# VectorE's order inside a visit: both masked copies, then the two steps of the turn back, then both row maxima

## The chip, the cores and the metric

The kernel runs on one core of one Trainium2 chip. The metric is the device time of one execution in microseconds. TensorE (PE in the profile) multiplies matrices, VectorE (DVE), ScalarE (ACT) and GpSimd (POOL) work on tiles element by element, and SyncE (SP) issues the transfers. Each engine takes its own instructions in order; across engines an instruction waits for a semaphore that another one raises.

## The reference

Four layers follow each other: a Fourier mixing layer, an attention layer, and the same two again. The change lies in the attention layer, `_B_ref`: 2048 rows of 640 numbers, 32 heads of 20, and each query sees itself and the 255 keys ahead of it.

```python
scores = jnp.einsum("bhqd,bhkd->bhqk", q, k) * (Dh ** -0.5)
mask = (idx[:, None] - idx[None, :] >= 0) & (idx[:, None] - idx[None, :] < W)   # W = 256
scores = jnp.where(mask[None, None], scores, -1e9)
p = _softmax(scores, axis=-1)
o = jnp.einsum("bhqk,bhkd->bhqd", p, v)
return (lambda x, *d: x.transpose(*d))(o, 0, 2, 1, 3).reshape(B, S, D) @ wo
```

## The kernel before

The queries are cut into 16 tiles of 128 rows. A query tile meets three key tiles: its own (near), the one ahead of it (near), and the one two ahead (far), of which only the part inside the window counts. Attention runs in *visits*, numbered G. A visit takes one query tile and four heads, in two halves `pi` of two heads each, and it works on several stages of different visits at once:

- `scores(G, ...)` on TensorE: the scores by query of this visit. The near ones go into the tiles sq (one for each half; `near` in the code), the far ones into the first quarter of the tiles sk (`farq`).
- `by_key(G - 8)` on TensorE: the scores of an earlier visit once more, by key, into the other three quarters of sk (`tps`).
- `largest(G, pi)` on VectorE: a masked copy (`copy_predicated`, line 1155) puts the far scores where the own tile's scores are masked; a row maximum (`tensor_reduce`, line 1157) over sq gives m.
- `probabilities(G - 8, pi)` on ScalarE: an activation of sk gives ptq (line 1210), first the half 1, then the half 0; GpSimd then masks it (lines 1214 and 1216).
- `part_tops` on GpSimd, at odd G: splits m into tops. `hand_on`, at odd G: TensorE turns the tops, ScalarE copies them out as ht (line 1175).
- `values`, at odd G: TensorE multiplies ptq with v; ScalarE copies the sums out as pvs (line 1242).
- `back(n)`, at even G from 12 on: the turn back. TensorE transposes pvs, VectorE takes a reciprocal r (line 1258) and a product o (line 1259), GpSimd splits o into two halves os (lines 1261 and 1262).
- a *fill unit* on TensorE at the end of most visits: 15 matmuls of a projection, of the output product or of the next layer. Their sums share two buffers, pf, with the turns and the values, and other engines evict them (the output product's by VectorE, line 935).
- single steps of layer norms on VectorE, let in by `slow_step` behind the last row maximum (`topped`).

So an even visit holds the turn back, and an odd visit the tops and the values. TensorE's order is the order of the code: each of its instructions is issued behind the one before. On VectorE, `in_line("dve")` issues an instruction behind the one noted last in `marks["dve"]`. What is not tied so (norm steps, evictions) is placed between by a scheduler when the program is built.

Of the kernel before, what the change touches and what calls it, by code (L numbers as in the profile page):

```python
# [72 lines left out]
def body(ctx: ExitStack, tc: tile.TileContext, x_in, cmat, whid, wqkv, wo, out):  # L73
# [750 lines left out]
    def attention(layer, proj, dst, final):  # L824
        with ExitStack() as st:
# [295 lines left out]
            @contextmanager  # L1121
            def in_line(name):
                with ExitStack() as order:
                    if name in marks:
                        order.enter_context(tc.issue_after(marks[name]))
                    yield
# [6 lines left out]
            def scores(G, which):  # L1133
# [3 lines left out]
                for a in which:  # L1137
# [4 lines left out]
                    for e in range(2):  # L1142
                        for pi in range(2):
                            r = slice(64 * pi, 64 * pi + 3 * DH + 2)
                            o = farq[pi][:, e] if a == 0 else near[pi][:, e, a % 2]
                            matmul(o, qs[r, p0 + e, t0:t0 + P], KS[kt // 2][r, p0 + e, k0:k0 + P], start=True, stop=True)

            def largest(G, pi):
                i, p0 = place(2 * G)
                n, k = divmod(G, 2)  # L1150
                if k == 0 and pi == 0:
                    TOP[n] = sb.tile([P, 2, 2, 2], F32, tag="m", name="m", bufs=3)
                far = farq[pi] if i >= 2 else neg[:, None, :].to_broadcast([P, 2, P])
                with in_line("dve"):
                    marks["dve"] = nc.vector.copy_predicated(near[pi][:, :, 0], mask[:, None, :].to_broadcast([P, 2, P]), far).ins  # L1155
                with in_line("dve"):
                    marks["dve"] = nc.vector.tensor_reduce(TOP[n][:, pi, :, k], near[pi][:, :, :1 + (i >= 1)], axis=AX.XY, op=OP.max).ins  # L1157
                topped[0] = marks["dve"]

            def part_tops(n):  # L1160

                m = TOP.pop(n).rearrange("p l e k -> p l (e k)")
                f = sb.tile([P, 2, 4], F32, tag="mf", name="mf", bufs=2)
                hl = tops[n % 2].rearrange("p (l h c) -> p l h c", l=2, h=2)
                nc.gpsimd.tensor_scalar(f, m, -1.0 / M_UP, None, op0=OP.mult)
                nc.gpsimd.tensor_copy(hl[:, :, 0], f)
                nc.gpsimd.tensor_tensor(hl[:, :, 1], f, hl[:, :, 0], op=OP.subtract)
# [76 lines left out]
            def back(n):  # L1244
                b, k = divmod(n, NP // 2)
                t = PVS.pop(n)
                pv = new_f().rearrange("p (a b) -> p a b", a=4)
                for m in range(2):
                    transpose(pv[:, 2 + m], t[:, m], idf)
                pbv = pv[:, 2:].rearrange("p m (h e) -> p (m h) e", e=32)  # L1250
                if k == 0:
                    flush(("out", b - 3))
                    OS[b] = sb.tile([P, 2, 2, D], F16, tag="os", name="os", bufs=3)
                r = sb.tile([P, 8], F32, tag="r", name="r", bufs=2)
                cs = slice(4 * k * DH, 4 * (k + 1) * DH)
                o = sb.tile([P, 2, 4 * DH], F32, tag="o", name="o", bufs=2)
                hi, lo = (OS[b][:, :, m, cs] for m in range(2))
                nc.vector.reciprocal(r, pbv[:, :, DH])
                nc.vector.tensor_tensor(o.rearrange("p m (h e) -> p (m h) e", e=DH), pbv[:, :, :DH],  # L1259
                                        r.unsqueeze(2).to_broadcast([P, 8, DH]), op=OP.mult)  # L1260
                nc.gpsimd.tensor_copy(hi, o)
                nc.gpsimd.tensor_tensor(lo, o, hi, op=OP.subtract)
                last = b == NBQ - 1
                d1 = (k + 1) * 4 * DH // P
                if last and d1 > k * 4 * DH // P and (d1 > 2 or k > LAST_FROM):
                    for m in range(2):
                        step0 = max(now[0] + LAST_STEPS[0], NG + 2 * KEY_LAG if m else LAST_STEPS[1] if d1 < ND else 0)
                        fill.append(Unit(step0, last_out(2 * b + m, lastd[0], d1), "last", NS + 2 * d1 + m, [(2 * b + m - 2, 2)]))
                    lastd[0] = d1
                elif k == NP // 2 - 1 and not last:  # L1270
                    for m in range(2):
                        i = 2 * b + m
                        at, due, kind = now[0] + OUT_STEPS[0] + OUT_STEPS[2] * m, 2 * NP * (b + 2) + OUT_STEPS[1], ("out", b)
                        need = [(i - 2, 2)] if i > 1 else []
                        outs.append((at, need, partial(out_turn, i)))
                        fill.append(Unit(at, out_tile(i), kind, due + 3 * m + 2, [(i, 1)] + ["wo"] * (layer == 0)))
# [38 lines left out]
            for G in range(NS // 2 + 1):  # L1315
                now[0] = g = 2 * G
                b, r = divmod(g, 2 * NP)
                if g == NG:
                    floor.append(loads[-1])
                if g < NG:  # L1320
                    if r == 0:
                        flush(("qk", b))
                        if b == 0:
                            queue_qk(1)
                            queue_v(1)
                keyed = 0 <= G - KEY_LAG < NG // 2
                if g < NG:
                    scores(G, (0,))
                if keyed:
                    by_key(G - KEY_LAG)  # L1330
                if g < NG:
                    scores(G, (2, 1))
                if g < NG:
                    largest(G, 0)
                if keyed:
                    probabilities(G - KEY_LAG, 1)
                if g < NG:
                    largest(G, 1)
                    if G % 2:
                        part_tops(G // 2)  # L1340
                if keyed:
                    probabilities(G - KEY_LAG, 0)
                n = due(G, HAND_LAG)
                if n is not None:
                    hand_on(n)
                n = due(G, BACK_LAG)
                if n is not None:
                    with in_line("dve"):
                        back(n)
                c = 2 if g == 0 else b + 3  # L1350
                if g < NG and c < NBQ and (g == 0 or r == X2_STEP):
                    wanted.append(c)
                if wanted and x2s and g >= x2s[0] + 4 * (g > 0):
                    slow.append(rows_norm(wanted.pop(0), x2s.pop()))
                    x2s.clear()
                if slow:
                    normed_at[0] = g
                if wanted and not slow and not x2s and g >= normed_at[0] + FREE_STEPS:
                    x2s += [g, [keep.tile([P, D], F32, tag="res0", name="x2", bufs=2) for t in range(2)]]
                    for t in range(2):  # L1360
                        load(x2s[1][t], x2_d[2 * wanted[0] + t])
                if g < NG and r == ROWS_STEP:
                    flush(("v", b))
                    if b < NBQ - 2:
                        proj.new_rows(b + 2)
                        queue_qk(b + 2)
                        queue_v(b + 2)
                if g < NG and r == HIDDEN_STEP:
                    if b == NBQ - 1 and not final:
                        flush(("v", b))  # L1370
                        hidden = Hidden(xu_d)
                        pieces = hidden.pieces()
                        for k in range(2):
                            fill.append(Unit(g + NEXT_STEPS[k], hidden.stage(k, None), "next", NG + k))
                for _ in range(STEPS[layer][G % 2]):
                    slow_step()
                run_later()
                for _ in range(PIECES):
                    next(pieces, None)
                while handed and handed[0][0] <= now[0]:  # L1380
                    handed.popleft()[1]()
                run_held(1 << 20)
                if outs and outs[0][0] <= g and all(done.get(k, 1 << 20) + FREE_STEPS <= g for k in outs[0][1]):
                    outs.pop(0)[2]()
                n = due(G, VALUE_LAG)
                if n is not None:
                    for part in range(2):
                        values(n, part)
                if not (G % 2 and NG - 2 * NP <= g < THIN_TO[layer]):
                    run_unit(G % 2 == 0)  # L1390
                if G % 2 and g < NG and left() and 2 * left() > must_to() - r:
                    run_unit()
# [40 lines left out]
```

## Time and profile before

| | us |
|---|---|
| median of three runs | 2076.37 (2076.05 to 2076.40) |
| the profiled execution's own time | 2078.21 |
| its span, first to last instruction | 2076.4 |
| TensorE busy | 1996.0 |
| VectorE busy | 1552.9 |
| masked copies, line 1155, 448 + 64 | 189.7 + 33.5 |
| row maxima, line 1157, 512 | 345.4 |
| reciprocals, line 1258, 128 | 25.3 |
| products o, line 1259, 128 | 40.8 |

A row of the timeline reads: start, duration, engine, line, operation, output <- input with shapes, count; in brackets the idle time of the engine ahead of it and what ended it. A row of the waits reads: who waited <- for whom: us in total, times, longest. A row of the stretches reads: from and to, length, and the busy time of TensorE, its weight loads, VectorE, ScalarE and GpSimd with their instruction counts, then granted clock, share of the DMA engines, and GB/s. The ends of matmuls are modelled in the trace.

### The profile page before, as it was taken

What the parts mean: (1) busy time and instruction counts of PE and PEld (TensorE: products, weight loads), DVE (VectorE), ACT (ScalarE), POOL (GpSimd) and SP (SyncE); (2) the same over time, 40 slices, a digit from 0 to 9 for tenths busy, and PEclk for the clock granted to TensorE, in tenths of its full rate; (3) what the DMA queues carried; (4) which work ended last, traced back from release to release, by engine and by line L of the source; (5) the groups of instructions that cost most, each with busy time, mean ns of one, the idle gap of its engine ahead of it and who ended that gap; (6) DMA issues with size and microseconds to landing.
All of it is one profiled execution on the core that took longest, in us unless ns stands there. A gap on an engine that the chain in (4) does not pass through costs nothing.

```text
span 2076.4 us, 55961 instructions
## 1 busy us (share of the span) xinstructions
PE 1996.0 (96%) x21881; PEld 1452.4 (70%) x21881; DVE 1552.9 (75%) x3261; ACT 1114.1 (54%) x1971; POOL 1471.0 (71%) x2162
## 2 busy tenths in 40 slices
PE   7999999999999999999999999999999999999998
PEld 4777777776767776777667777777677677777765
DVE  8888778767688788766638779787777877776673
ACT  5444555534256666666654444444342666666664
POOL 5777788868458778765557778777783677776654
PEclk9999999999999999999999999999999999999999
DMA  7556467565554444443635455454845454543322
GB/s 271 182 200 207 159 216 237 169 254 193 141 107 118 109 109 117 98 102 91 175 131 175 159 174 183 149 171 144 298 146 131 92 124 106 128 110 88 85 74 71
DMA packets 280509, 311.11 MB, mean 150 GB/s; under 512 B 107572, under 2 KB 214836, under 8 KB 271156
## 3 DMA queue, kind: packets, MB, share of 16 engines
q1 hardware_dynamic: 279668, 306.88, 49.9%
q8 instruction: 171, 2.80, 0.6%
q14 instruction: 94, 0.77, 0.1%
q10 hardware_dynamic: 576, 0.66, 0.1%
HBM read 201.72 MB, written 83.46 MB: 137 GB/s over the span
## 4 chain that ended last, share of the span: by engine, by line
PE 63%; DVE 16%; issue 6%; ACT 5%; POOL 5%; DMA 4%; SPq 0%; DVEq 0%; POOLq 0%; ACTq 0%
PE pf L126 28%; PE y L126 11%; PE x L126 10%; PE z L126 7%; PE sk L126 5%; DVE cc L536 4%; DVE sq L1155 3%; DVE m L1157 2%; ACT ptq L1210 2%; PE sq L126 2%; DMA res<-accd 2%; DVE res L559 1%; DVE lnt L151 1%; POOL cs L526 1%; DVE lnst L139 1%
## 5 line engine op out<-in xcount | busy, mean ns | idle before, releaser
L126 PEld LDWEIGHTS <-cc 128*128 128x128 f16 x5376 | 524.4, 98 | 214.8 <-issue 15.1
L1210 ACT ACTIVATE ptq<-sk,shift,alpha 128x768 f32<-128x768 f32 (+2 forms) x512 | 469.3, 944 | 111.0 <-DVE x L935 55.0
L126 PEld LDWEIGHTS <-big 128*128 128x128 f16 x4320 | 415.0, 98 | 129.6 <-issue 29.5
L1157 DVE TENSOR_REDUCE m<-sq 128x2 f32<-128x512 f32 (+1 forms) x512 | 345.4, 675 | 25.8
L1155 DVE COPY_PREDICATED sq<-mask,sk 128x256 f32<-128x256 int32 x448 | 189.7, 423 | 144.4 <-PE sq L126 138.1
L533 ACT ACTIVATE cc<-cs 128x512 f16<-128x512 f32 x256 | 153.6, 623 | 262.6 <-POOL cs L526 150.3
L126 PE MATMUL pf<-early,big 128*128 128x256 f16 x2400 | 289.2, 274 | 4.4 <-ACT ht L1175 3.7
L1214 POOL TENSOR_SCALAR_AFFINE_SELECT ptq<-ptq 128x512 f32<-128x512 f32 x224 | 144.3, 644 | 183.1 <-ACT ptq L1210 180.8
L126 PE MATMUL y<-zc,cc 128*128 128x320 f16 x1728 | 262.8, 299 | 3.2 <-DVE pf L559 3.2
L536 DVE SCALAR_TENSOR_TENSOR cc<-cs,cc 128x512 f16<-128x512 f32 x256 | 248.1, 978 | 6.9 <-ACT cc L533 6.8
L536 DVE SCALAR_TENSOR_TENSOR cc<-cq,cc 128x512 f16<-128x512 f32 x192 | 207.1, 1080 | 0.1
L126 PE MATMUL pf<-ptq,v 128*32 128x128 f32 (+1 forms) x3840 | 183.6, 329 | 10.1 <-DVE o L1259 3.5
L126 PE MATMUL z<-zc,cc 128*128 128x320 f16 x1152 | 177.7, 299 | 7.0 <-DVE res L559 7.0
L126 PE MATMUL x<-zc,cc 128*128 128x320 f16 x1152 | 177.7, 299 | 0.0
L1216 POOL TENSOR_SCALAR_AFFINE_SELECT ptq<-ptq 128x512 f32<-128x512 f32 x256 | 164.9, 644 | 13.0 <-ACT ptq L1210 12.8
L126 PEld LDWEIGHTS pf<-ptq,v 128*32 128x32 f32 x3840 | 114.8, 110 | 56.0 <-PE pf L126 7.7
L365 ACT ACTIVATE qf<-pf 128x256 f32<-128x256 f32 x160 | 60.9, 381 | 166.7 <-PE pf L126 128.7
L126 PE MATMUL pf<-big,early 128*128 128x320 f16 x960 | 141.0, 299 | 2.2 <-ACT ht L1175 1.3
L525 POOL TENSOR_TENSOR cs<-cq 128x512 f32<-128x512 f32 x64 | 86.6, 1354 | 69.8 <-DVE cc L536 69.1
L126 PEld LDWEIGHTS <-qs 62*128 62x128 f16 x2688 | 87.7, 94 | 59.1 <-issue 57.9
L126 PE MATMUL pf<-bo,ot 128*128 128x320 f16 x840 | 123.5, 299 | 4.6 <-DVE x L935 2.6
L126 PEld LDWEIGHTS <-ot 128*128 128x128 f16 x960 | 91.9, 98 | 46.6 <-issue 9.4
(141 smaller groups left out, 3505.4 us busy)
## 6 DMA issues: line engine op xcount, KB each, us to landing
cq<-in_cmat_dram SPq DMA_DIRECT2D x64, 1024.0 KB
accd<-res SPq DMA_DIRECT2D x96, 320.0 KB
res<-accd SPq DMA_DIRECT2D x96, 320.0 KB
x<-x2d SPq DMA_DIRECT2D x64, 320.0 KB
qkd<-early SPq DMA_DIRECT2D x160, 128.0 KB
ks<-qkd SPq DMA_DIRECT2D x108, 160.0 KB
qs<-qkd SPq DMA_DIRECT2D x84, 160.0 KB
x2d<-res SPq DMA_DIRECT2D x32, 320.0 KB
```

The costliest lines, as they stand in the source:

```text
L126: i = getattr(nc.tensor, what)(*args, **kw)
L139: nc.vector.bn_stats(st[:, h], x[:, h * 320:(h + 1) * 320])
L151: ts(u, g, g, h, op0=OP.mult, op1=OP.mult)
L365: nc.scalar.activation(f, pf[:, :QB], AF.Copy, scale=down)
L525: g.tensor_tensor(s1, a21, a22, op=OP.add)
L533: nc.scalar.activation(cc[m][:, 0], f, AF.Copy, scale=C_UP)
L536: nc.vector.scalar_tensor_tensor(cc[m][:, 1], f, C_UP, cc[m][:, 0], op0=OP.mult, op1=OP.subtract)
L1155: marks["dve"] = nc.vector.copy_predicated(near[pi][:, :, 0], mask[:, None, :].to_broadcast([P, 2, P]), far).ins
L1157: marks["dve"] = nc.vector.tensor_reduce(TOP[n][:, pi, :, k], near[pi][:, :, :1 + (i >= 1)], axis=AX.XY, op=OP.max).ins
L1210: marks["act"] = nc.scalar.activation(o[:, pi], tps[pi][:, :, first:], AF.Sigmoid, bias=shift, scale=alpha[:, 0:1]).ins
L1214: nc.gpsimd.affine_select(out=q[:, :, a0], in_=q[:, :, a0], pattern=[[0, 4], [-1, P]], base=0, channel_multiplier=1, compare_op=OP.is_gt, ...
L1216: ins = nc.gpsimd.affine_select(out=q[:, :, a0 + 2], in_=q[:, :, a0 + 2], pattern=[[0, 4], [1, P]], base=0, channel_multiplier=-1, compare ...
```

## The change

`largest` is split: the masked copy becomes a function of its own, `masked`. Both copies of a visit come first, then the turn back if the visit has one, then both row maxima. The product o is noted in `marks["dve"]`, so the row maxima are issued behind it.

```diff
+            def masked(G, pi):
+                i, p0 = place(2 * G)
+                far = farq[pi] if i >= 2 else neg[:, None, :].to_broadcast([P, 2, P])
+                with in_line("dve"):
+                    marks["dve"] = nc.vector.copy_predicated(near[pi][:, :, 0], mask[:, None, :].to_broadcast([P, 2, P]), far).ins
+
             def largest(G, pi):
...
-                far = farq[pi] if i >= 2 else neg[:, None, :].to_broadcast([P, 2, P])
-                with in_line("dve"):
-                    marks["dve"] = nc.vector.copy_predicated(near[pi][:, :, 0], mask[:, None, :].to_broadcast([P, 2, P]), far).ins
                 with in_line("dve"):
                     marks["dve"] = nc.vector.tensor_reduce(TOP[n][:, pi, :, k], near[pi][:, :, :1 + (i >= 1)], axis=AX.XY, op=OP.max).ins
...
-                nc.vector.tensor_tensor(o.rearrange("p m (h e) -> p (m h) e", e=DH), pbv[:, :, :DH],
-                                        r.unsqueeze(2).to_broadcast([P, 8, DH]), op=OP.mult)
+                marks["dve"] = nc.vector.tensor_tensor(o.rearrange("p m (h e) -> p (m h) e", e=DH), pbv[:, :, :DH],
+                                                       r.unsqueeze(2).to_broadcast([P, 8, DH]), op=OP.mult).ins
...
                 if g < NG:
-                    largest(G, 0)
+                    masked(G, 0)
                 if keyed:
                     probabilities(G - KEY_LAG, 1)
                 if g < NG:
-                    largest(G, 1)
-                    if G % 2:
-                        part_tops(G // 2)
+                    masked(G, 1)
+                n = due(G, HAND_LAG)
                 if keyed:
                     probabilities(G - KEY_LAG, 0)
-                n = due(G, HAND_LAG)
                 if n is not None:
                     hand_on(n)
                 n = due(G, BACK_LAG)
                 if n is not None:
                     with in_line("dve"):
                         back(n)
+                if g < NG:
+                    for pi in range(2):
+                        largest(G, pi)
+                    if G % 2:
+                        part_tops(G // 2)
```

How the instructions then stand on VectorE in an even visit of the first layer, about a third of the way in. The names in brackets are the semaphores that an instruction waits for: PE, Activation (ScalarE), Pool (GpSimd), DVE itself, or a DMA queue. sq_6968 and sk_6970 are the tiles of half 0, sq_6969 and sk_6971 those of half 1. Before:

```order
L1155 COPY_PREDICATED sq_6968<-mask,sk_6970 128x256 [waits PE_49,Activation_49]
L1157 TENSOR_REDUCE m<-sq_6968 128x2 [waits DVE_49,Pool_49]
L1155 COPY_PREDICATED sq_6969<-mask,sk_6971 128x256 [waits PE_49,Activation_49]
L1157 TENSOR_REDUCE m<-sq_6969 128x2 [waits DVE_49]
L1258 RECIPROCAL r<-pf 128x8 [waits PE_49]
L139 BN_STATS lnst<-x_9483 128x6
L1259 TENSOR_TENSOR o<-pf,r 128x160 [waits DVE_49,Pool_49]
L142 BN_AGGR lnmv<-lnst 128x2 [waits DVE_49]
L935 SCALAR_TENSOR_TENSOR x_9045<-pf,beta,x_9045 128x320 [waits DMAHW0_49,PE_49]
```

The same visit on VectorE with the change:

```order
L1152 COPY_PREDICATED sq_6968<-mask,sk_6970 128x256 [waits PE_49,Activation_49]
L1152 COPY_PREDICATED sq_6969<-mask,sk_6971 128x256 [waits PE_49,Activation_49]
L1261 RECIPROCAL r<-pf 128x8 [waits PE_49]
L1262 TENSOR_TENSOR o<-pf,r 128x160 [waits DVE_49,Pool_49]
L1160 TENSOR_REDUCE m<-sq_6968 128x2
L1160 TENSOR_REDUCE m<-sq_6969 128x2
L139 BN_STATS lnst<-x_9483 128x6
L935 SCALAR_TENSOR_TENSOR x_9045<-pf,beta,x_9045 128x320 [waits DMAHW0_49,PE_49]
L142 BN_AGGR lnmv<-lnst 128x2 [waits DVE_49]
```

The second copy moved ahead of the first maximum, and it waits for the same two engines as before; r and o moved ahead of both maxima; the norm step that stood between r and o now stands behind them. On TensorE, where the near scores of a visit begin (they overwrite the tiles that the row maxima of the visit before have read), before:

```order
L126 LDWEIGHTS qs
L126 MATMUL sq_6968<-ks,qs 128x128
L126 LDWEIGHTS qs
L126 MATMUL sq_6969<-ks,qs 128x128 [waits DVE_49]
L126 LDWEIGHTS qs
```

and with the change:

```order
L126 LDWEIGHTS qs
L126 MATMUL sq_6968<-ks,qs 128x128 [waits DVE_49]
L126 LDWEIGHTS qs
L126 MATMUL sq_6969<-ks,qs 128x128 [waits DVE_49]
L126 LDWEIGHTS qs
```

Nothing moved on TensorE; the first near product now has a wait of its own for VectorE, the second had one already.

## Prediction

> **What bounds the kernel now.** The change touches the two attention layers alone. I read the granted clock first (0.998, so nothing is lost there), then a stretch in the middle of a layer, then the waits of TensorE, then single visits in the timeline.
>
> ```profile
> core 0: 2076.4 us, clock 0.998
> 800.00:900.00 100.00, 96.45 (x1500) 71.81 (x1492) 73.80 (x174) 66.09 (x106) 73.63 (x163) 1.00 0.48 115
> ```
>
> In these 100 us TensorE (second column) is busy 96.45 us, VectorE (fourth) 73.80. TensorE's order, which the change leaves alone, sets the time; VectorE matters only where TensorE waits for it. How often it does, first in 610 to 1030 us, then in 1620 to 2040 us:
>
> ```profile
> PE sk L126 <- ACT ptq L1210: 2.8, 5, 1.6
> PE pf L126 <- ACT ht L1175: 2.2, 3, 0.9
> PE pf L126 <- DVE o L1259: 2.1, 5, 0.7
> PE pf L126 <- DVE x L935: 2.0, 5, 0.6
> PE sq L126 <- DVE m L1157: 0.2, 1, 0.2
> ...
> PE sk L126 <- ACT ptq L1210: 2.5, 9, 0.5
> PE pf L126 <- DVE x L935: 1.9, 5, 0.6
> PE pf L126 <- ACT ht L1175: 1.8, 3, 0.9
> PE pf L126 <- DVE o L1259: 1.4, 4, 0.6
> PE sq L126 <- DVE m L1157: 1.0, 2, 0.8
> ```
>
> The change could at best remove the o rows, 3.5 us. So the question is whether it keeps the rows "PE sq <- DVE m" as small as they are. One even visit and the start of the next:
>
> ```profile
> 712.23 0.39 PE L126 MATMUL sq<-ks,qs 62*128 62x128 f16 x8
> 712.49 1.87 ACT L1210 ACTIVATE ptq<-sk,shift,alpha 128x768 f32<-128x768 f32 x2
> 712.72 0.43 DVE L1155 COPY_PREDICATED sq<-mask,sk 128x256 f32<-128x256 int32 x1
> 713.25 0.69 DVE L1157 TENSOR_REDUCE m<-sq 128x2 f32<-128x512 f32 x1
> 713.86 0.42 DVE L1155 COPY_PREDICATED sq<-mask,sk 128x256 f32<-128x256 int32 x1
> 714.31 0.69 DVE L1157 TENSOR_REDUCE m<-sq 128x2 f32<-128x512 f32 x1
> 714.92 0.20 DVE L1258 RECIPROCAL r<-pf 128x8 f32<-128x8 f32 x1
> 715.41 0.39 PE L126 MATMUL sq<-ks,qs 62*128 62x128 f16 x8
> 715.53 0.31 DVE L1259 TENSOR_TENSOR o<-pf,r 128x160 f32<-128x160 f32 x1
> 715.62 0.99 ACT L1210 ACTIVATE ptq<-sk,shift,alpha 128x768 f32<-128x768 f32 x1 [1.26 <-DVE x L935]
> ```
>
> The second row maximum ends at 714.31 + 0.69 = 715.00; the next visit's near scores overwrite its bank from 715.41. **The slack is 0.41 us**, and this is the median of the even visits in both layers. An odd visit has more: its second maximum starts at 709.97, ends at 710.66, and the sq above starts at 712.23, 1.57 us later.
>
> ```profile
> 709.97 0.69 DVE L1157 TENSOR_REDUCE m<-sq 128x2 f32<-128x512 f32 x1
> ```
>
> **The change part by part.** It removes and adds no instruction. In every visit the second copy moves ahead of the first maximum; in even visits reciprocal and product also move ahead of both maxima. TensorE's and SyncE's rows stand as before, so no DMA is passed. On GpSimd the cast of o moves one or two places forward, into time in which GpSimd waits for o anyway, so I cost it at nothing:
>
> ```profile
> POOL os L1261 <- DVE o L1259: 38.4, 47, 7.5
> ```
>
> ScalarE's few swaps touch single activations: nothing too.
>
> First term, *the second copy now waits for ScalarE.* The order listing shows it waiting for Activation before and after. The activation is the visit's first ptq, which reads the other part of the tile sk that this copy reads. Today 1.14 us lie between the two copies' starts, so the wait has almost always passed. Where it had not, it can be seen:
>
> ```profile
> 640.11 1.85 ACT L1210 ACTIVATE ptq<-sk,shift,alpha 128x768 f32<-128x768 f32 x2
> 641.12 0.43 DVE L1155 COPY_PREDICATED sq<-mask,sk 128x256 f32<-128x256 int32 x1 [1.34 <-ACT ptq L1210]
> ...
>   ACT ptq L1210: 2.6, 4
> ```
>
> The first ptq takes 0.99 us (row at 715.62), so it ended at 641.10 and the copy began 0.02 later. I went through the visits with far tiles: no second copy begins before the first ptq has ended, and the smallest distance is this 0.02. In the quoted visit the first ptq ends at 712.49 + 0.99 = 713.48. The first copy is over at 713.15, so the second, which could start at 712.72 + 0.32 = 713.04, starts at 713.51. That is 0.35 earlier than today, but VectorE has stood idle for 0.36, time that the first maximum filled.
>
> The Trainium skill bears on this wait: PSUM — Partial Sum Buffer, section "PSUM bank collisions raise a hardware error", says that two engines may not touch one bank in the same partitions at once, reads against reads included. By that rule the wait cannot be argued away and the sum is the one below; if the 0.02 were only VectorE's own order, the sum would be that of the fourth rival. The trace agrees with the rule in every visit.
>
> Second term, *the rest of the chain.* After the second copy now stand reciprocal, product, maximum, maximum. Their distances, start to start, come from these neighbours:
>
> ```profile
> 618.48 0.42 DVE L1155 COPY_PREDICATED sq<-mask,sk 128x256 f32<-128x256 int32 x1
> 618.80 0.21 DVE L152 TENSOR_SCALAR lnt<-lnt 128x1 f32<-128x1 f32 x1
> ...
> 634.30 0.20 DVE L1258 RECIPROCAL r<-pf 128x8 f32<-128x8 f32 x1
> 634.60 0.33 DVE L1259 TENSOR_TENSOR o<-pf,r 128x160 f32<-128x160 f32 x1
> ...
> 783.45 0.32 DVE L1259 TENSOR_TENSOR o<-pf,r 128x160 f32<-128x160 f32 x1
> 783.69 0.54 DVE L935 SCALAR_TENSOR_TENSOR x<-pf,beta,x 128x320 f32<-128x320 f32 x1
> ```
>
> Copy to an independent step 0.32; reciprocal to product 0.30; product to an independent step 0.24; maximum to the next step 0.61 (713.25 to 713.86); the last maximum 0.69. Sum 2.16 us. The second maximum would end at 713.51 + 2.16 = 715.67 instead of 715.00. **It moves by 0.67 us against a slack of 0.41**, so TensorE stands for 0.26. No distance here was seen for exactly these pairs: the lower bound drops 0.10 (0.23 for the product, no wait tail), the upper takes whole durations, 0.42 + 0.30 + 0.33 + 0.69 + 0.69 = 2.43. I take 2.16, since the quoted neighbours overlap as these would.
>
> The Trainium skill would take the upper one: VectorE: DVE Perf Modes, section "The DRAIN you can't avoid", says the next operation does not start before the pipe has emptied. The trace differs: the maximum of 713.25 lasts to 713.94 and the next copy starts at 713.86.
>
> Third term, *how often.* Queued behind TensorE's waiting sq product are the transposes of the tops, the values and the next fill unit: everything, so a stall there is lost unless a later wait gives it back. I counted the even visits that hold both the moved steps and a far tile, from the sq starts (first and last of each kind):
>
> ```profile
> 611.10 0.39 PE L126 MATMUL sq<-ks,qs 62*128 62x128 f16 x8
> 2026.88 0.42 PE L126 MATMUL sq<-ks,qs 62*128 62x128 f16 x8
> ...
> 631.61 0.39 PE L126 MATMUL sq<-ks,qs 62*128 62x128 f16 x8
> 1959.93 0.39 PE L126 MATMUL sq<-ks,qs 62*128 62x128 f16 x8
> 1962.71 0.42 PE L126 MATMUL sq<-ks,qs 62*128 62x128 f16 x8
> ...
> 624.11 0.39 PE L126 MATMUL sq<-ks,qs 62*128 62x128 f16 x8
> 1991.28 0.42 PE L126 MATMUL sq<-ks,qs 62*128 62x128 f16 x8
> ```
>
> - 69 visits about 3.2 us long (611.10 to 2026.88): 0.26 each, 17.9 us.
> - 22 visits about 2.8 us long, whose fill unit is a narrow one (631.61 to 1959.93; 1962.71 - 1959.93 = 2.78): slack 0.01, so 0.66 each, 14.5 us.
> - 15 visits in which ScalarE begins its first ptq late (624.11 to 1991.28), by my sums from 0.4 to 1.4, mean 0.65: 9.8 us.
>
> Together 42.2 us. For odd visits I add nothing: the wait for the first ptq lets their chain end some 0.15 later, on a slack above 1 us.
>
> Fourth term, *what is given back.* A stall ahead of hp and values lets ScalarE and VectorE catch up, so the waits for o, ht, x and ptq in the following odd visit shrink by at most the stall. Visit by visit, the smaller of the two adds to 5.4 us in the first layer and 4.6 in the second. Bounds: 0, and all eight rows of those kinds, 16.7.
>
> Sum: 42.2 - 10.0 = +32 us. The profiled execution's span is 2076.4, its own time 2078.21 with 1.8 around the span; the runs' median, 2076.37, lies at the span. So 2076.4 + 32 = **2108 us**.
>
> **The rivals.**
>
> 1. *More is given back* (2092). The stall of each even visit gives ScalarE 0.26 us before the next ptq, the late kind vanishes (-9.8) and all 16.7 is absorbed: 42.2 - 9.8 - 16.7 = 16. For it: late visits follow backlogs on ScalarE. Against: the stall delays the first copy too, and the second ptq waits for that copy. Chance 0.15.
> 2. *The chain is longer* (2137). Whole durations add 0.27 in 106 visits, 28.6 us. Evictions of x and norm steps also follow the maxima, so values could wait for x more than today's 3.9. Against: the overlap of 0.08 seen above. Chance 0.15.
> 3. *Faster: the fill buffers come back early* (2072). The product ends near 714.4 instead of 715.84, so the 3.5 us of waits for o and the 1.2 us for m go. It decides from the point where the second maximum moves by less than 0.41; for that the chain would have to be 0.26 shorter. Against: the 22 short visits have no slack at all. Chance 0.04.
> 4. *The second copy does not wait* (2080). It starts at 713.04, the maximum ends at 715.20, inside the slack; only the short visits lose (0.19 x 22 = 4) and the late ones about 4, less half given back. Against: the 0.02 above. Chance 0.06.
>
> **How the numbers follow.** The forecast holds 0.60, about 2098 to 2120 by itself. With rivals 1 and 2 to either side the range is 2086 to 2132. What a measurement of this kernel can tell from no change is about 0.2%, 4.2 us. Faster: 0.04. Within: 0.04, most of rival 4. Slower: 0.92.
>
> **What would show it.** Waits of "PE sq <- DVE m" should grow from the 1.2 us above to some 35 to 45 us; "DVE sq <- ACT ptq" from 2.6 us in 4 to 38 us (106 x 0.36) or more; "PE pf <- DVE o" should be gone. Even visits of 3.18 us should read about 3.44. If the second copy starts before the first ptq ends, the first term is wrong; if it waits but TensorE does not, the slack was more than I read.

## The result, and the profile after

| | before | with the change |
|---|---|---|
| median of six runs each, us | 2076.80 | 2110.41 |
| lowest and highest, us | 2076.05 to 2079.60 | 2107.49 to 2110.99 |
| span of the profiled execution, us | 2076.4 | 2108.7 |

The ratio of the means is 1.0156, with a 95% interval of 1.0143 to 1.0169. The medians differ by 33.6 us and the spans of the two profiled executions by 32.3, and the prediction said 32. In the experiments further down, one execution (the profiled one of the turn back alone with ht free) was granted a clock of 0.588 and took 3411.59 us, and neither its time nor its trace is used. Here is the same even visit as in the prediction, in the timeline after the change.

```profile
716.06 0.39 PE L126 MATMUL sq<-ks,qs 62*128 62x128 f16 x8
716.31 1.87 ACT L1213 ACTIVATE ptq<-sk,shift,alpha 128x768 f32<-128x768 f32 x2
716.55 0.43 DVE L1152 COPY_PREDICATED sq<-mask,sk 128x256 f32<-128x256 int32 x1 [0.30 <-PE sq L126]
717.34 0.43 DVE L1152 COPY_PREDICATED sq<-mask,sk 128x256 f32<-128x256 int32 x1 [0.36 <-ACT ptq L1213]
717.67 0.20 DVE L1261 RECIPROCAL r<-pf 128x8 f32<-128x8 f32 x1
717.98 0.32 DVE L1262 TENSOR_TENSOR o<-pf,r 128x160 f32<-128x160 f32 x1
718.22 1.28 DVE L1160 TENSOR_REDUCE m<-sq 128x2 f32<-128x512 f32 x2
719.24 0.69 PE L126 MATMUL sq<-ks,qs 62*128 62x128 f16 x8
```

The second copy waits 0.36 us for the first ptq and starts 1.28 us after the near scores. From its start to the end of the second maximum (718.22 + 1.28 = 719.50) pass 2.16 us. The next near scores begin on time, at 719.24, 3.18 us after the last ones; but their second product needs the bank that the second maximum reads. So the eight products take 0.69 us instead of 0.39: TensorE stands for 0.30 us inside this row. The waits of TensorE in 610 to 1030 us, then in 1640 to 2060 us:

```profile
PE sq L126 <- DVE m L1160: 6.5, 18, 0.4
PE pf L126 <- ACT ht L1178: 4.9, 4, 1.8
PE pf L126 <- DVE x L935: 2.9, 6, 0.9
PE sk L126 <- ACT ptq L1213: 1.6, 3, 1.3
...
PE sq L126 <- DVE m L1160: 6.0, 17, 0.4
PE pf L126 <- ACT ht L1178: 5.5, 5, 1.8
PE pf L126 <- DVE x L935: 2.5, 4, 0.9
PE sk L126 <- ACT ptq L1213: 1.1, 6, 0.3
```

The rows for m have grown from 0.2 and 1.0, those for o are gone, and those for ht, which I had not expected to move, have grown from 2.2 and 1.8. **The rows for m show only a part of the stall.** The end of a matmul is modelled, and a product that is held up behind another one shows as idle time only beyond that end. In the visit above the row of eight is longer and no idle time is noted. For the 224 visits with far tiles I took the time from the start of the first near product to the end of the eighth, beyond 0.39 us: together 41.1 us after and 3.1 before. VectorE's own waits show where it begins:

```profile
DVE sq L1152 <- PE sq L126: 169.3, 151, 3.6
DVE sq L1152 <- ACT ptq L1213: 58.2, 129, 1.9
```

The second row was 2.6 us in 4.

To see where the 32.3 us of the span lie, I measured each visit from the turns on TensorE (of pvs in even visits, of the tops in odd ones), and compared visit by visit. Even visits 12 to 126 grew by 38.4 us in both layers together, with a median of 0.31. Odd visits shrank by 2.7 together; the rest, -3.5, lies in the visits ahead of these, which hold no turn back (2.9 of it in the first layer); why is not shown. Within the odd visits eight grew by 10.9 together (numbers 33, 47, 63 and 79 of each layer); without them the odd ones gave back 13.6. One of the eight, 33 of the first layer, after the change:

```profile
672.00 1.08 DVE L166 TENSOR_SCALAR lny<-x,lnmv,lnt 128x640 f32<-128x640 f32 x1
673.12 0.74 ACT L177 ACTIVATE rx<-lny 128x640 f16<-128x640 f32 x1 [1.39 <-DVE lny L166]
673.76 1.85 ACT L1213 ACTIVATE ptq<-sk,shift,alpha 128x768 f32<-128x768 f32 x2
675.51 0.25 ACT L1178 ACTIVATE ht<-pf 16x128 f16<-16x128 f16 x1
...
675.81 1.80 PE L126 MATMUL pf<-early,big 128*128 128x256 f16 x15 [1.85 <-ACT ht L1178]
```

and the same visit before:

```profile
670.72 0.56 DVE L166 TENSOR_SCALAR lny<-x,lnmv,lnt 128x640 f32<-128x640 f32 x1
671.32 0.74 ACT L177 ACTIVATE rx<-lny 128x640 f16<-128x640 f32 x1
671.96 0.97 ACT L1210 ACTIVATE ptq<-sk,shift,alpha 128x768 f32<-128x768 f32 x1
672.84 0.25 ACT L1175 ACTIVATE ht<-pf 16x128 f16<-16x128 f16 x1
672.99 0.97 ACT L1210 ACTIVATE ptq<-sk,shift,alpha 128x768 f32<-128x768 f32 x1
```

Two things have changed here. First, the norm step lny on VectorE comes later. Before, it stood between r and o; now it stands behind both row maxima. Counted from the turn of the tops on TensorE, it ends 0.6 to 1.0 us later in all eight, and rx and the ptq behind it on ScalarE wait for it. It also took longer, 1.08 us instead of 0.56, for a reason that no run here shows. Second, the scheduler has put ht behind both ptq instead of between them. The fill unit needs the buffer that ht empties, and TensorE stood 1.85 us. By the start times, ht stood behind both ptq of its visit in 12 of the 120 odd visits 9 to 127 before the change and in 17 after it; of the eight, the two numbered 47 had it so before.

### The profile page after: what moved, and what is told of

It is laid out like the page before. It is cut to its first block, busy times and chain, and to the rows that moved or that the text cites. A ratio compares the mean times of both kernels' runs of the same rounds, so it can differ in the third digit from the quotient of the medians.

```text
span 2108.7 us, 55813 instructions
## 1 busy us (share of the span) xinstructions
PE 2012.2 (95%) x21881; PEld 1450.6 (69%) x21881; DVE 1532.8 (73%) x3261; ACT 1125.3 (53%) x1971; POOL 1468.1 (70%) x2162
## 4 chain that ended last, share of the span: by engine, by line
PE 61%; DVE 21%; ACT 7%; issue 4%; DMA 4%; POOL 2%; SPq 0%; DVEq 0%; ACTq 0%; POOLq 0%
PE pf L126 24%; PE y L126 12%; PE x L126 11%; PE z L126 8%; DVE m L1160 7%; ACT ptq L1213 5%; PE sk L126 3%; DVE cc L536 3%; DVE sq L1152 3%; PE sq L126 2%; DVE o L1262 1%; DVE lnt L151 1%; DMA res<-accd 1%; DVE res L559 1%; DVE lnt L152 1%
## 5 line engine op out<-in xcount | busy, mean ns | idle before, releaser
L126 PEld LDWEIGHTS <-cc 128*128 128x128 f16 x5376 | 523.9, 98 | 214.7 <-issue 14.6
L1160 DVE TENSOR_REDUCE m<-sq 128x2 f32<-128x512 f32 (+1 forms) x512 | 318.9, 664 | 0.0
L126 PEld LDWEIGHTS <-qs 62*128 62x128 f16 x2688 | 93.2, 94 | 94.1 <-issue 88.8
L126 PEld LDWEIGHTS pf<-ptq,v 128*32 128x32 f32 x3840 | 109.9, 110 | 52.8 <-DVE x L935 6.9
L126 PE MATMUL sq<-ks,qs 62*128 62x128 f16 x1792 | 109.5, 216 | 19.9 <-DVE m L1160 12.9
```

Source lines behind the costliest of these rows:

```text
L126: i = getattr(nc.tensor, what)(*args, **kw)
```

## The experiments

The theory to test has two parts: the second copy, put next to the first, waits for ScalarE's first ptq; and the row maxima come out later by that wait and by r and o, of which 0.41 us fit into the slack of a long visit. The main rivals: the wait as such is the price, or the number of steps ahead of the maxima is.

Times are compared through their ratio to the kernel before, which ran beside each; its median was 2075.09 to 2075.67 us beside the experiments and 2076.80 beside the change. A ratio is one of means, so the medians can give a slightly different one. Each trace is of one execution, so the sums by visits can be some us off the difference of the medians.

| order on VectorE in an even visit | ht | ratio | 95% interval | median us |
|---|---|---|---|---|
| copy, copy, r, o, max, max (the change) | free | 1.0156 | 1.0143 to 1.0169 | 2110.41 |
| copy, copy, max, max, r, o | free | 1.0059 | 1.0046 to 1.0072 | 2087.63 |
| copy, max, copy, r, o, max | free | 1.0058 | 1.0043 to 1.0073 | 2088.27 |
| copy, r, o, copy, max, max | free | 0.9989 | 0.9980 to 0.9998 | 2072.36 |
| the change | tied | 1.0093 | 1.0080 to 1.0107 | 2094.67 |
| as before | tied | 0.9968 | 0.9956 to 0.9980 | 2068.93 |
| copy, max, copy, r, o, max | tied | 0.9989 | 0.9976 to 1.0002 | 2074.47 |
| copy, r, o, copy, max, max | tied | 0.9940 | 0.9928 to 0.9952 | 2063.09 |
| the same, odd visits as before | tied | 0.9951 | 0.9936 to 0.9965 | 2065.97 |
| the change, halves of ptq swapped | tied | 1.0160 | 1.0145 to 1.0175 | 2109.27 |

### Both copies first, the turn back left behind

Against the kernel before:

```diff
-                    largest(G, 0)
+                    masked(G, 0)
                 if keyed:
                     probabilities(G - KEY_LAG, 1)
                 if g < NG:
-                    largest(G, 1)
+                    masked(G, 1)
+                    largest(G, 0)
+                    largest(G, 1)
```

> Both copies ahead of both row maxima, the turn back left behind them as in the kernel before. My theory: the second copy still waits for the first ptq, so it starts 1.28 us after the near scores begin; 0.32 + 0.61 + 0.69 later the second maximum ends, at 2.90 instead of 2.77. 0.13 us fit in the slack of 0.41, so only the short visits pay: 22 x 0.13 = 3 us, and the turn back comes 0.13 later for perhaps 1 us more. 2080 us, waits of the second copy for ptq 40 us or more. Rival (the wait for ScalarE as such is the price, whatever follows it): half or more of the 33.6 us, 2093 or above. Rival (the wait is nothing, placing r and o early is the price): 2076.

Measured: 2087.63 us, +0.59%. Both rivals fall, but 8 us more than my theory were lost. The second maximum ends 2.90 us after the near scores begin, in the median of the even visits, as expected, and the visits' own median did not grow: there the row maxima fit into the slack. The waits of the second copy for ptq came to 70.9 us, and by themselves they cost far less than the 33.6. TensorE's waits over the whole execution name only a part of the loss:

```profile
PE sk L126 <- ACT ptq L1213: 10.3, 17, 3.2
PE pf L126 <- DVE o L1262: 8.8, 19, 0.8
PE sq L126 <- DVE m L1160: 2.3, 5, 1.0
```

Waits for o were 3.5 us before, those for ptq 9.5 and those for m 5.3. Here r and o come after the later maxima, and in 69 of 128 visits a norm step or an eviction still stands between them. The largest single losses lie in visits 14, 24 and 25 of the first layer, 5.0 us together; in 24 the far scores wait 3.2 us for ptq, 1.6 before. That waits for o have grown is shown; how the rest divides stays open.

### The turn back alone, ahead of the second maximum

Against the change:

```diff
                 if g < NG:
                     masked(G, 0)
+                    largest(G, 0)
                 if keyed:
                     probabilities(G - KEY_LAG, 1)
...
                         back(n)
                 if g < NG:
-                    for pi in range(2):
-                        largest(G, pi)
+                    largest(G, 1)
                     if G % 2:
                         part_tops(G // 2)
```

> Copy, maximum, copy, then the turn back, then the second maximum: only r and o are moved, and the second copy keeps its old distance of 1.14 us from the first, so it does not wait for ptq. My theory: the second maximum ends 0.32 + 0.30 + 0.24 - 0.45 = 0.41 later, just the slack; long visits pay 0 to 0.05 (2 us), short ones 0.41 (9 us), late ones about 3; waits for o worth 3.5 go. ScalarE's order has the same five displaced ht as the full change, worth up to 6. 2084 to 2090 us. Rival (r and o early are the whole price): 2110. Rival (the wait for ScalarE is the whole price): 2073 to 2076.

Measured: 2088.27 us (the median of four executions), ratio 1.0058, inside the range of my theory and far from both rivals. No trace of it is read here, so this shows a price and not yet where it lies. The same order was then run with ht tied; the edit that ties it is shown further down.

> Copy, maximum, copy, turn back, second maximum, with ht tied; to be held against the kernel before with ht tied (0.9968 of the kernel before, 2069 us). Only r and o are moved and the second copy does not have to wait. My theory: the second maximum ends 0.41 us later than before, which is the whole slack of a long visit, so the even visits' median grows by 0.05 us or less, while the short ones grow by 0.41 (9 us in all); waits for o, 3.7 us, go. 2074 to 2079 us, and waits of the second copy for ptq under 5 us. If the price of placing r and o ahead of a maximum were more than the slack's overrun: 2085 or above. If no step ahead of the maxima cost anything without the wait for ptq: 2066 to 2069.

Measured: 2074.47 us, 0.9989 against the 0.9968 of the kernel before with ht tied: +0.21%, 4.4 us. The two intervals just overlap, so the size of this is rough. The even visits' median grew by 0.05 and the 22 short ones by 9.1 us together, both as expected. The waits of the second copy for ptq came to 8.0 us, where I had expected under 5, and those of TensorE for o are gone. An even visit in its timeline:

```profile
711.39 0.39 PE L126 MATMUL sq<-ks,qs 62*128 62x128 f16 x8
711.64 1.87 ACT L1214 ACTIVATE ptq<-sk,shift,alpha 128x768 f32<-128x768 f32 x2
713.02 0.42 DVE L1152 COPY_PREDICATED sq<-mask,sk 128x256 f32<-128x256 int32 x1
713.34 0.20 DVE L1262 RECIPROCAL r<-pf 128x8 f32<-128x8 f32 x1
713.65 0.33 DVE L1263 TENSOR_TENSOR o<-pf,r 128x160 f32<-128x160 f32 x1
713.89 0.68 DVE L1160 TENSOR_REDUCE m<-sq 128x2 f32<-128x512 f32 x1
714.57 0.44 PE L126 MATMUL sq<-ks,qs 62*128 62x128 f16 x8
```

The second copy starts long after the first ptq has ended, without a wait. The second maximum ends at 714.57, 3.18 us after the near scores began and 0.41 later than before: just when the next ones begin, which then take 0.44 instead of 0.39. The slack is used up to the last and hardly exceeded.

### The turn back in the time of the wait

Against the change:

```diff
                 if keyed:
                     probabilities(G - KEY_LAG, 1)
+                n = due(G, BACK_LAG)
+                if n is not None:
+                    with in_line("dve"):
+                        back(n)
                 if g < NG:
                     masked(G, 1)
...
-                n = due(G, BACK_LAG)
-                if n is not None:
-                    with in_line("dve"):
-                        back(n)
```

> The same steps as in the change, but r and o stand between the two copies, in the time in which the second copy would wait. My theory: the second copy starts 1.40 us after the near scores begin (first copy at 0.49, +0.32, +0.30, +0.24), 0.12 after ptq has ended, the second maximum ends at 3.02 instead of 2.77: 0.25 later, inside the slack for long visits, 0.24 x 22 = 5 us for short ones; o-waits of 3.5 go, displaced ht add up to 6. 2079 to 2085 us, waits of the second copy for ptq below 15 us. Rival (the number of steps ahead of the maxima is the price, wherever they stand): 2110.

Measured: 2072.36 us, 0.9989, better than my range of 2079 to 2085. The same six instructions of VectorE as in the change, in another order, and the whole loss of 33.6 us is gone. The same visit:

```profile
713.86 0.39 PE L126 MATMUL sq<-ks,qs 62*128 62x128 f16 x8
714.11 1.87 ACT L1213 ACTIVATE ptq<-sk,shift,alpha 128x768 f32<-128x768 f32 x2
714.35 0.43 DVE L1152 COPY_PREDICATED sq<-mask,sk 128x256 f32<-128x256 int32 x1
714.68 0.20 DVE L1261 RECIPROCAL r<-pf 128x8 f32<-128x8 f32 x1
714.99 0.33 DVE L1262 TENSOR_TENSOR o<-pf,r 128x160 f32<-128x160 f32 x1
715.23 0.42 DVE L1152 COPY_PREDICATED sq<-mask,sk 128x256 f32<-128x256 int32 x1
715.56 1.28 DVE L1160 TENSOR_REDUCE m<-sq 128x2 f32<-128x512 f32 x2
717.04 0.39 PE L126 MATMUL sq<-ks,qs 62*128 62x128 f16 x8
```

r and o run while ScalarE finishes the first ptq (714.11 + 0.99 = 715.10), and the second copy starts 1.37 us after the near scores, without idle time. The second maximum ends at 716.84, 0.20 ahead of the next near scores, which take their 0.39. The even visits' median did not grow at all, and the short ones grew by 5.6 us together (5 expected). What my range did not have is that the odd visits shrank by 8.0 us, more than what I had counted for o; why is not shown. The waits of the second copy for ptq still come to 33.7 us in 77, where I had expected fewer than 15: those are mostly odd visits, in which nothing stands between the copies. I had left them out. Further down the odd visits go back to their old order, those waits fall to 8.6 us (with ht tied), and no gain can be told, which speaks once more against the wait as such being the price.

### ht tied between the two ptq

Against the kernel before (the changed kernel gets the same order of the two):

```diff
-                nc.scalar.activation(ht, hp, AF.Copy)
+                with in_line("act"):
+                    marks["act"] = nc.scalar.activation(ht, hp, AF.Copy).ins
...
-                if keyed:
-                    probabilities(G - KEY_LAG, 0)
                 n = due(G, HAND_LAG)
                 if n is not None:
                     hand_on(n)
+                if keyed:
+                    probabilities(G - KEY_LAG, 0)
```

In the changed kernel:

> The change with ScalarE's copy ht tied between the two ptq of its visit. In the change five of these copies more than before stand behind both ptq, and the waits of TensorE for ht grew from 5.8 to 12.0 us. My theory: this is a side effect worth about 6 us, 2104 us, and the waits of the near scores for the row maxima stay. Rival (the wait for ht only takes the place of another): 2110.

Measured: 2094.67 us, 1.0093. The tie took off 0.63%, 13 us, twice what I expected; the rows of near products still hold 42.4 us beyond their length (41.1 without the tie), so the stalls for the row maxima are a thing of their own. The waits for ht fell from 12.0 to 3.1 us. In the kernel before:

> The kernel before, with ScalarE's copy ht tied between the two ptq of its visit (there 20 of 128 stand behind both). Tying it took 16 us off the changed kernel. Theory A: most of this gain is there without the change too, since TensorE waits 5.8 us for ht here and about as much again follows from it; 2066 us, and the displaced ht explain only some 6 us of the change's 33.6. Theory B: the displaced ht are the change's own doing and half of its loss; then tying changes little here, 2074 to 2076.

Measured: 2068.93 us, 0.9968. Between the two theories: tying is worth 0.32% there. So with ht tied in both kernels the change costs 1.0093 / 0.9968 - 1 = 1.25% (26 us), and 0.31% (6 us) of its 1.56% come from ht being displaced more often. The intervals of the ratios make either figure uncertain by about 0.2%.

In the eight odd visits the displaced ht is not all: tied in both kernels, they still grew by 6.1 us instead of 10.9. There the late norm step remains, with a wait of TensorE of 0.5 to 1.0 us in each. In four of them it is the values that wait, for the eviction x, which stands behind the late lny on VectorE; before, with ht tied, these waits were 0.15:

```profile
850.91 1.51 PE L126 MATMUL pf<-ptq,v 128*32 128x256 f32 x32 [0.92 <-DVE x L935]
```

With the turn back between the copies:

> The turn back between the two copies, and ht tied. Theory: the two effects add; 2072.4 less 6 to 10, so 2063 to 2067 us, with waits for the row maxima at 2 us as without the tie. If the tie matters only where the near scores stall: 2072.

Measured: 2063.09 us, 0.9940. The time is that of effects that add, at the low end of the range, though the waits for the row maxima came to 3.6 us and not 2 (4.9 without the tie). This is 0.6% faster than the kernel before; against the kernel before with ht tied it is 0.28%. With odd visits in their old order:

> The turn back between the two copies in even visits, odd visits as in the kernel before (copy, maximum, copy, maximum), ht tied. Theory: odd visits have over 1 us of slack, so their order is worth nothing; the same time as with the turn back between the copies and odd visits reordered, within 2 us. If the second copy's wait in odd visits delays ScalarE or the row maxima further on: faster than that by 3 us or more.

Measured: 2065.97 us, 0.9951, within the interval of the one above. The order in odd visits is worth nothing that can be told here.

### The halves of ptq swapped

In the change with ht tied, `probabilities` runs half 0 first and half 1 second. Its new third argument says which of the two calls is the second one; GpSimd's masks follow that one.

```diff
                 if keyed:
-                    probabilities(G - KEY_LAG, 1)
+                    probabilities(G - KEY_LAG, 0, False)
...
                 if keyed:
-                    probabilities(G - KEY_LAG, 0)
+                    probabilities(G - KEY_LAG, 1, True)
```

> The change with ht tied (2094.7 us) and ScalarE's two ptq in the other order, half 0 first. The second copy of a visit then has no ptq of its own visit ahead of it; in its place the first ptq waits for the first copy, 0.67 us later than now, and the second for the second copy. My theory: the second maximum ends at 2.97 us after the near scores begin, so long visits no longer stall there and short ones 0.19; but the second ptq ends at about 2.88, after the next far scores want its bank (2.76 in long visits, 2.36 in short ones): 69 x 0.12 + 22 x 0.52 + some 5 = 25 us in place of 37; 2080 to 2090 us, waits of the second copy for ptq near 0, waits of the far scores for ptq above 15 us. Rival (that wait costs nothing, the number of steps ahead of the maxima does): 2095 or more.

Measured: 2109.27 us, 1.0160, against 1.0093 without the swap: slower where I expected 5 to 15 us faster. The number would fit the rival, its trace does not. TensorE's waits over the execution, then one visit:

```profile
PE pf L126 <- ACT ht L1179: 31.2, 88, 1.0
PE sk L126 <- ACT ptq L1214: 22.1, 42, 0.9
PE sq L126 <- DVE m L1160: 2.6, 7, 1.0
...
715.55 0.39 PE L126 MATMUL sq<-ks,qs 62*128 62x128 f16 x8
716.04 0.76 DVE L1152 COPY_PREDICATED sq<-mask,sk 128x256 f32<-128x256 int32 x2 [0.46 <-PE sq L126]
716.56 1.87 ACT L1214 ACTIVATE ptq<-sk,shift,alpha 128x768 f32<-128x768 f32 x2 [0.90 <-DVE sq L1152]
717.26 1.28 DVE L1160 TENSOR_REDUCE m<-sq 128x2 f32<-128x512 f32 x2
718.28 0.48 PE L126 MATMUL sk<-ks,qs 62*128 62x128 f16 x4
718.89 0.42 PE L126 MATMUL sq<-ks,qs 62*128 62x128 f16 x8
```

VectorE does what I said: the copies stand next to each other, the second maximum ends at 718.54, 2.99 us after the near scores, and the waits for m are down to 2.6 us. But ScalarE first stands idle for 0.90 us and begins its ptq 1.01 us after the near scores instead of some 0.25, and I had priced only the far scores that wait for its second ptq. In odd visits ht, between the ptq, is late as well, and the fill unit waits for it: 31.2 us. Odd visits grew by 25.5 us and even ones by 19.0 over the kernel before with ht tied. The wait was taken from one engine and came back, larger, through another.

## Why the prediction was right

Held against the prediction's steps, in its order:

- **The second copy waits for ScalarE: right.** In the visit shown it starts 1.28 us after the near scores (predicted 1.28) with 0.36 us of idle time (0.36). With r and o in that time the loss is gone. The rule of PSUM — Partial Sum Buffer in the Trainium skill (section "PSUM bank collisions raise a hardware error") fits the traces: in the visits with far tiles, no copy of a half overlaps a ptq of the same half in any of the ten traces used, and no second copy begins sooner than 0.03 us after its ptq has ended. These waits are semaphores of the program, and no run here takes them out.
- **The rest of the chain is 2.16 us: right**, to the hundredth in the visit shown (717.34 to 719.50). The upper bound by whole durations, 2.43, did not show: a copy of 0.43 us is followed by r 0.33 after its start. The prediction read too little of VectorE: DVE Perf Modes in the Trainium skill (section "The DRAIN you can't avoid") when it had the skill take that bound. The section goes on that a next operation that is not held starts earlier, and the early starts here do not go against that.
- **The overrun of the slack: right, with sizes slightly off.** The 69 long visits grew by 18.7 us (17.9 predicted), with a median of 0.31 instead of 0.26; the 22 short ones by 13.5 (14.5); those in which ptq begins late, 16 by the trace, by 6.9 (9.8), and the other nine lost 0.7. Even visits together come to 38.4 us instead of 42.2. The dose shows the slack itself. The second maximum came 0.20 us later with the turn back in the wait, 0.41 with the turn back alone (ht tied in both kernels), and 0.67 with the change; the long visits' medians grew by 0.00, 0.05 and 0.31, and those of the short ones, which have 0.01 us of slack, by 0.20, 0.41 and 0.62.
- **What is given back: too small.** Odd visits without the eight shrank by 13.6 us; I had said 10.0, and 16.7 as a bound.
- **Odd visits and ScalarE's swaps at nothing: wrong.** The eight odd visits grew by 10.9 us. Some 5 of these go with ht tied in both kernels, in which the change costs 26 us instead of 32. In the order listing the swaps were single rows; the price was in who waits for ht, a fill buffer and so TensorE, and I had not asked that. The other 6 lie where the norm step comes late, moved from between r and o to behind the maxima, and with it what stands behind it on VectorE and ScalarE. The waits in the traces show this path; no run moves the norm step alone. My second rival named norm steps and evictions behind the maxima, but the sum did not have them.

These errors nearly cancel: 38.4 + 10.9 - 13.6 - 3.5 = 32.2, where the 3.5 lie in the visits ahead of number 12, which the prediction did not price. So the mechanism was right, but that the total of 32 came out so close is partly luck.

Of the signs that I named, the waits for ptq (58.2 us, 38 or more expected) and the end of the waits for o came as said. The row "PE sq <- DVE m" came to 12.5 us in the two stretches instead of 35 to 45, not since the stall was smaller but since this row does not show all of it. Rival 1 was nearer on the giving back, but its late visits did not vanish: they grew. The point of rival 3, a shift smaller than the slack, was reached by another order: the turn back in the wait is faster than before by 0.11% (interval 0.02 to 0.20%), and by 0.60% with ht tied.

## What to carry to other kernels

Before moving an independent instruction away from between two others, look at what the second of these waits for on another engine: the one between may have been the cover for that wait, and the place where cover is missing is the place for the steps that one wants early. Price a later result by the slack up to its reader, visit kind by visit kind: here, in visits with 0.41 us of slack, 0.20 us later was free, 0.41 nearly so, and 0.67 cost 0.31, while visits with 0.01 of slack paid nearly all of it. And follow each small swap that a scheduler makes, on another engine or behind the moved steps, to whoever waits for it.

## What the runs showed that was not expected

A stall of TensorE inside a run of matmuls is found in the length of the run (0.69 us instead of 0.39), while the waits named a fraction of it (14.6 us of some 41). In visit 33 TensorE waited 1.85 us for a ScalarE copy of 0.25 us that stood behind both ptq, and 0.97 us in the same visit with the copy tied between them: the place behind one more activation of 0.97 us cost 0.9.
